# A tuned attention and SwiGLU kernel: waits at its end for the last stores alone, and 11 warming products in place of 13

## The chip, the cores and the metric

The kernel runs on one core of one Trainium2 chip. The metric is device time in microseconds; where several runs are told of, their median stands. A profile shows one further execution, its span running from its first to its last instruction. The engines are called PE (TensorE, products; PEld are its weight loads), ACT (ScalarE), DVE (VectorE), POOL (GpSimd) and SP (SyncE). SP issues nearly all DMAs; POOL issues those that add to what lies in memory.

## The reference

There are 2048 rows x of width 1024 in bfloat16. They are normalised, pass through linear attention with 32 heads of 32, and through a gated feed-forward block of inner width 3584; the result is x plus their product with a SiLU:

```python
xn  = layernorm(x)
q, k, v = heads(xn @ wqkv)                 # 32 heads of 32
pq, pk  = phi(q), phi(k)                   # phi(t) = (t+1 if t>0 else exp(t)) + 1e-6
kv  = einsum("bhsd,bhse->bhde", pk, v);  z = sum over s of pk
o   = (pq @ kv) / (pq . z + 1e-6)
s   = o.reshape(S, D) @ wo
h   = (silu(xn @ w_gate) * (xn @ w_up)) @ w_down
out = x + s * silu(h)
```

## The kernel before, in words

The kernel is not written in the order in which it runs. The builder makes a list of operations (class Op: engine, function, estimated time, what it reads and writes), and a planner (class Plan) orders it.

*The work.* All large products are done on 2 x 2 blocks with seven block products in place of four times two, and some blocks are split once more in the same way. The rows are cut into tiles of 128, normalised on DVE, POOL and ACT (ln_tile) and transposed (t_tile): the first four tiles on PE with ACT copying the result into X, the later ones by transposing DMAs. Keys and values come first, with the sums kv and z kept in PSUM; then the gate, up and query products in blocks of 512 columns; then the attention's output, written to s_scratch; last the down projection in four groups of rows. The inner values h are kept in h_scratch in DRAM, with some sums made by accumulating DMAs.

*The start.* DVE clears a small tile wz, POOL makes the identity matrix, and PE computes NWARM products of the identity with wz, 512 columns each. Their results are not used. They go around the eight PSUM banks. Behind them on PE stand the transposes of row tile 0 (L237), which read the tile that DVE normalises (L755), and then the first true products (p_piece, L230). These read the transposed tile from X, which ACT copies there (L358), and chunks of the QKV weights from H, which SP loads with the first DMAs of all (L371).

*The end.* The first three groups of the down projection add their results to the output by accumulating DMAs from POOL (dacc), out of three buffers in turn (g_ring), each with a semaphore. The output had been filled with x for them. The last group adds x on DVE and stores the sum with plain DMAs from SP, each of its stores with a semaphore of its own. Its last output tile is cut into pieces of 256, 128 and 128 columns.

*The planner.* Every operation has a due time, worked out backwards from its readers and from PE's cumulative estimated time (pecum). For loads that have a reader, the due time also decides which PE operation must have run before the load is issued. PE's operations run in the listed order within a window of ten; the other engines take, among what is ready, the one with the earliest due time, less a boost. The table BOOST gives boosts by the operation's number in the list. Each PE operation's estimate counts in two ways: with the mm_cost at which it was made in pecum, and with its field busy in the simulated clock.

*Emission.* Plan.emit turns the order into one program per engine, in which an operation stands behind the waits that its engine does not already know to be met. A wait is emitted as wait_ge by _run (L222); every operation raises a semaphore, its engine's by one or its DMA's own by 16. Plan.count has the last value of each semaphore. When all is ordered, the builder adds waits to SP's program: one for each DMA semaphore in use, in the order in which the semaphores were made, for the value in Plan.count. At the end of the block all engines meet (L254). The five programs are straight lines without loops.

Of the kernel before, what the change touches and what calls it, by code (L numbers as in the profile page):

```python
# [237 lines left out]
    return last  # L238


def build_kernel(nc, A_x, A_wqkv, A_wo, B_w_gate, B_w_up, B_w_down, out, WINDOW=10, NWARM=13, NPE=4, LEAD=16.0, CLAMP=1000.0, AHEAD=4.0):
    S, D, FF = 2048, 1024, 3584
    NT, KT, NG, NPAIR = 16, 8, 8, 14
    EPS_LN, EPS_PHI = 1e-5, 1e-6
# [9 lines left out]
    with ExitStack() as es:  # L254
# [20 lines left out]
        def named(*key):  # L275
            return Region([key])
# [6 lines left out]
        ident, ones, maskbd = (TM.at(14 * KB + 256 * q, 256, FP16) for q in range(3))  # L283
# [16 lines left out]
        ps = [es.enter_context(nc.psum_tensor("ps%d" % b, [128, 512], F32)) for b in range(8)]  # L300
        bank_r = [named("bank", b) for b in range(8)]
# [29 lines left out]
        semn = {}  # L331
# [6 lines left out]
        PL = Plan(WINDOW, LEAD, CLAMP, AHEAD)  # L338
        MM = 0.2137

        def mm_cost(mms):
            return sum(max(r.shape[-1] / 2400.0 + 0.0026, 0.03) * (o.shape[0] * r.shape[0] / 16384.0)
                       for (o, _, r, _, _) in mms)

        def pe_mm(reads, writes, mms):
            return PL.op("pe", reads, writes, partial(_mm_group, mms), mm_cost(mms))
# [60 lines left out]
        ident_r, ones_r, mask_r = (TM.reg(14 * KB + 256 * q, 256) for q in range(3))  # L407
# [72 lines left out]
        wz = TM.at(0, 1 * KB, FP16)  # L480
        wz_r = TM.reg(0, 1 * KB)
        dve([], [wz_r], lambda h: h.memset(wz, 0.0), 256)
        for n in range(NWARM):
            b = n % 8
            pe_mm([ident_r, wz_r], [bank_r[b]], [(ps[b][:, :], ident[:, :], wz, True, True)]).busy = 0.38


        XOF = {1: "R00", 2: "R10", 3: "R11", 4: "T4", 5: "T1", 6: "T2", 7: "T3"}
# [1150 lines left out]
        sp = {}  # L1639
# [81 lines left out]
        for g, c in enumerate(G):  # L1721
# [5 lines left out]
        feed(None)  # L1727
        flush()

        BOOST = {1: 5058, 29: 18306, 30: 754, 31: 18202, 32: 872, 33: 880, 34: 881, 37: 3, 39: 68, 41: -2586,  # L1730
# [7 lines left out]
        for k, v in BOOST.items():  # L1738
            PL.ops[k].boost = v
        PL.schedule()  # L1740
        prog = PL.emit(esem)
        for s in semn.values():
            if id(s) in PL.count:
                prog["sp"].append(("w", s, PL.count[id(s)]))

        @block.tensor
        def _(h):
# [19 lines left out]
def bass_recurrent_scan__linear_attn_block__swiglu_ffn__prompt_kernel(  # L1767
    nc: bass.Bass,
    A_x: bass.AP,
    A_wqkv: bass.AP,  # L1770
    A_wo: bass.AP,
    B_x: bass.AP,
    B_w_gate: bass.AP,
    B_w_up: bass.AP,
    B_w_down: bass.AP,
    out: bass.AP,
):
    build_kernel(nc, A_x, A_wqkv, A_wo, B_w_gate, B_w_up, B_w_down, out)
# [28 lines left out]
```

## Time and profile before

| | |
|---|---|
| median of 3 runs | 705.55 us (705.12 to 705.91) |
| profiled execution, its own time | 704.51 us |
| its span, first to last instruction | 702.7 us |
| PE busy | 694.8 us (99%) |
| DVE busy | 610.7 us (87%) |
| ACT busy | 424.7 us (60%) |
| POOL busy | 68.4 us (10%) |
| DMA | 103.68 MB, mean 148 GB/s |

In the profile, a line of the code such as L230 is often that of a helper: all products are recorded at L230, all transposes on PE at L237, all ACT operations at L358, SP's DMAs at L371 and POOL's at L375. Groups are told apart by the tiles that they write and read, as in out_dram<-W. The busy time counts no waits and no issues of DMAs, so an engine that executes nothing but waits is idle in it. A time of 5.24 us in a row is measured from the start of the span.

### The profile page before, as it was taken

How to read it: one execution, taken by the hardware profiler on the slowest of the kernel's cores; microseconds unless marked ns; L12 is line 12 of the kernel's file. 1: busy time of each engine (PE TensorE's matmuls, PEld its weight loads, DVE VectorE, ACT ScalarE, POOL GpSimd, SP SyncE). 2: the span in 40 equal slices, each digit the busy share in tenths (PEclk: the TensorE clock that was granted, in tenths of full speed). 3: DMA queues.
4: the chain of work that ended last, by engine and by line, in shares of the span. 5: the costliest groups of instructions: out<-in, count | busy, mean ns of one | idle time of the engine just before them, and what ended most of it. 6: DMA issues, size and time to landing. Idle time of an engine off the chain costs nothing.

```text
span 702.7 us, 11996 instructions
## 1 busy us (share of the span) xinstructions
PE 694.8 (99%) x4436; PEld 421.4 (60%) x4436; DVE 610.7 (87%) x1391; ACT 424.7 (60%) x848; POOL 68.4 (10%) x87
## 2 busy tenths in 40 slices
PE   8999999999999999999999999999999999999996
PEld 3544445555555566666666666666665448687784
DVE  6999998667999799898999999888879998768685
ACT  4877645867978967868866567775763113232222
POOL 2111000001100011020110110001101211111010
PEclk9999999999999999999999999999999999999999
DMA  9434213126612376584670486766627875666672
GB/s 313 106 83 106 54 60 121 61 90 145 155 61 69 117 195 169 174 236 101 166 194 1 106 242 198 242 218 165 165 81 225 192 182 176 155 165 156 207 180 69
DMA packets 96107, 103.68 MB, mean 148 GB/s; under 512 B 18256, under 2 KB 91344, under 8 KB 95952
## 3 DMA queue, kind: packets, MB, share of 16 engines
q1 hardware_dynamic: 84976, 92.43, 41.9%
q0 software_dynamic: 11072, 10.49, 11.9%
q8 instruction: 35, 0.57, 0.3%
q14 instruction: 24, 0.20, 0.1%
HBM read 65.54 MB, written 37.36 MB: 146 GB/s over the span
## 4 chain that ended last, share of the span: by engine, by line
PE 99%; ACT 0%; POOL 0%; DVE 0%; issue 0%; POOLq 0%
PE ps L230 99%; PE ps L237 0%; ACT X L358 0%; DVE W L368 0%; POOL TM L415 0%; ACT W L358 0%; POOL TM L414 0%; POOLq L1792 0%
## 5 line engine op out<-in xcount | busy, mean ns | idle before, releaser
L358 ACT ACTIVATE TM<-ps 128x512 f32<-128x512 f32 (+2 forms) x341 | 169.0, 528 | 50.5 <-PE ps L230 45.6
L368 DVE TENSOR_TENSOR ps<-ps,TM 128x256 f32<-128x256 f32 (+1 forms) x322 | 157.7, 509 | 40.2 <-PE ps L230 35.8
L230 PE MATMUL ps<-X,W 128*128 128x512 f16 (+1 forms) x896 | 190.4, 340 | 0.0
L230 PE MATMUL ps<-P,W 128*128 128x512 f16 (+1 forms) x896 | 188.9, 338 | 0.0
L358 ACT ACTIVATE H<-ps 128x512 f16<-128x512 f32 (+1 forms) x181 | 106.3, 601 | 55.9 <-PE ps L230 54.9
L230 PEld LDWEIGHTS ps<-X,W 128*128 128x128 f16 (+1 forms) x896 | 87.5, 98 | 59.5 <-DVE W L368 0.2
L230 PEld LDWEIGHTS ps<-P,W 128*128 128x128 f16 (+1 forms) x896 | 87.6, 98 | 58.4 <-DVE ps L368 0.2
L358 ACT ACTIVATE ps<-ps 128x256 f32<-128x256 f32 (+2 forms) x149 | 63.5, 426 | 72.5 <-PE ps L230 70.9
L230 PE MATMUL ps<-H,X 128*128 128x512 bf16 (+4 forms) x556 | 104.8, 336 | 0.5 <-ACT X L358 0.5
L368 DVE TENSOR_TENSOR H<-H 128x1024 f16<-128x1024 f16 (+5 forms) x150 | 87.1, 598 | 10.6 <-ACT H L358 8.4
L368 DVE TENSOR_TENSOR W<-W 128x256 f16<-128x256 bf16 (+6 forms) x256 | 89.1, 388 | 5.1 <-PE ps L230 2.9
L230 PE MATMUL ps<-W 128*128 128x256 f16 x512 | 90.0, 273 | 0.0
L368 DVE TENSOR_TENSOR TM<-ps,TM 128x512 f32<-128x512 f32 x99 | 67.8, 686 | 12.5 <-PE ps L230 11.5
L230 PEld LDWEIGHTS ps<-H,X 128*128 128x128 f16 x556 | 52.8, 98 | 41.6 <-ACT X L358 0.6
L375 POOL DMA_DIRECT2D h_scratch<-H x28 | 33.7, 1283 | 437.4 <-DVE H L368 197.0
L230 PEld LDWEIGHTS ps<-W 128*128 128x128 f16 (+1 forms) x512 | 50.0, 98 | 27.3 <-ACT TM L358 0.6
L230 PE MATMUL ps<-H,W 128*128 128x512 f16 (+2 forms) x280 | 63.6, 358 | 0.0
L230 PE MATMUL ps<-H 128*128 128x256 f16 (+4 forms) x432 | 60.9, 273 | 0.0
L230 PE MATMUL ps<-W,H 128*128 128x256 f16 (+1 forms) x314 | 53.5, 305 | 0.0
L358 ACT ACTIVATE H<-TM 128x512 f16<-128x512 f32 x61 | 38.3, 631 | 15.6 <-DVE TM L368 15.0
L230 PEld LDWEIGHTS ps<-H 128*128 128x128 f16 (+1 forms) x432 | 38.3, 98 | 14.6 <-ACT H L358 0.2
L368 DVE TENSOR_TENSOR H<-ps,TM 128x512 f16<-128x512 f32 (+1 forms) x59 | 40.3, 685 | 2.7 <-PE ps L230 2.5
(92 smaller groups left out, 552.1 us busy)
## 6 DMA issues: line engine op xcount, KB each, us to landing
h_scratch<-H SPq DMA_DIRECT2D x70, 256.0 KB, 3.2
X<-h_scratch SPq DMA_DIRECT2D x15, 896.0 KB, 5.2
W<-in_B_w_gate_dram SPq DMA_DIRECT2D x7, 1024.0 KB, 5.4
W<-in_B_w_up_dram SPq DMA_DIRECT2D x7, 1024.0 KB, 6.1
h_scratch<-H POOLq DMA_DIRECT2D x28, 256.0 KB, 5.7
H<-in_B_w_down_dram SPq DMA_DIRECT2D x8, 896.0 KB, 6.7
W<-in_A_x_dram SPq DMA_DIRECT2D x16, 256.0 KB, 3.1
H<-in_A_wqkv_dram SPq DMA_DIRECT2D x8, 512.0 KB, 7.9
```

Source lines behind the costliest of these rows:

```text
L230: last = h.matmul(o, l, r, start=st, stop=sp, skip_group_check=True)
L358: op = PL.op("act", reads, writes, lambda h: h.activation(o, i, func, **kw), nel(o) / 1200.0 + (0.055 if src == "ps" else 0.095))
L368: return dve(reads, writes, lambda h: h.tensor_tensor(o, a, b, op), nel(o), 1.92 if fast else 0.96)
L375: return PL.op("pool", reads, writes, lambda h: h.dma_start(o, i, accum_op=ALU.add), 1.0, sem=s, nbytes=2 * nbytes)
```

## The change

The parameter NWARM goes from 13 to 11. The estimate of each warming product is raised in the same ratio, and PE's cumulative time is set after them to what 13 gave. The keys of BOOST behind the warming products go down by two, with the same values, since there are two operations fewer ahead of them. So all other operations are planned in the same order.

At the end, SP no longer waits for every DMA semaphore. The builder goes through the planned order and keeps, for each semaphore, the last DMA that no other operation in the list depends on, moved to the end of the table each time; SP then waits for these alone, with the value that the semaphore has after that DMA. A DMA that some operation depends on was waited for by that operation, or by one that its engine knows to be behind it.

```diff
-def build_kernel(..., WINDOW=10, NWARM=13, NPE=4, LEAD=16.0, CLAMP=1000.0, AHEAD=4.0):
+def build_kernel(..., WINDOW=10, NWARM=11, NPE=4, LEAD=16.0, CLAMP=1000.0, AHEAD=4.0):
...
         for n in range(NWARM):
             b = n % 8
-            pe_mm([ident_r, wz_r], [bank_r[b]], [(ps[b][:, :], ident[:, :], wz, True, True)]).busy = 0.38
+            pe_mm([ident_r, wz_r], [bank_r[b]], [(ps[b][:, :], ident[:, :], wz, True, True)]).busy = 0.38 * 13 / NWARM
+        PL.pecum = 13 * (512 / 2400.0 + 0.0026)
...
-        BOOST = {1: 5058, 29: 18306, 30: 754, 31: 18202, ...
+        BOOST = {1: 5058, 27: 18306, 28: 754, 29: 18202, ...
...
         prog = PL.emit(esem)
-        for s in semn.values():
-            if id(s) in PL.count:
-                prog["sp"].append(("w", s, PL.count[id(s)]))
+        ends = {}
+        for o in PL.order:
+            if o.sem is not None and not o.succs:
+                ends.pop(id(o.sem), None)
+                ends[id(o.sem)] = o.ev
+        for s, _, val, _ in ends.values():
+            prog["sp"].append(("w", s, val))
```

More of the change, by code (lines that the diff above doesn't have):

```diff
@@ L238, in _tr_group, with build_kernel @@
     return last
-def build_kernel(nc, A_x, A_wqkv, A_wo, B_w_gate, B_w_up, B_w_down, out, WINDOW=10, NWARM=13, NPE=4, LEAD=16.0, CLAMP=1000.0, AHEAD=4.0):
+def build_kernel(nc, A_x, A_wqkv, A_wo, B_w_gate, B_w_up, B_w_down, out, WINDOW=10, NWARM=11, NPE=4, LEAD=16.0, CLAMP=1000.0, AHEAD=4.0):
     S, D, FF = 2048, 1024, 3584
@@ L1728, in build_kernel @@
         flush()
-        BOOST = {1: 5058, 29: 18306, 30: 754, 31: 18202, 32: 872, 33: 880, 34: 881, 37: 3, 39: 68, 41: -2586,
[7 rows of a table removed]
+        BOOST = {1: 5058, 27: 18306, 28: 754, 29: 18202, 30: 872, 31: 880, 32: 881, 35: 3, 37: 68, 39: -2586, 40: 6519, 44: 4544, 47: 3050, 49: 459, 58: 181, 76: 407, 78: 3, 102: 60, 115: 570, 121: 103, 140: 3, 150: 3, 159: -3, 164: 60, 165: 150, 205: 60, 226: 8, 284: -20, 301: 60, 710: 8, 970: 8, 1059: 60, 1112: 174, 1310: 1408, 1941: 60, 1943: 3, 1949: 60, 1963: 146, 2027: 357, 2051: 150, 2315: 8, 2324: 20, 2328: 8, 2441: 76, 2456: 3, 2483: 3, 2558: 74, 2574: 3, 3352: 860, 3354: 867, 3409: 542, 3421: 238, 3471: 2362, 3495: 360, 3505: 8, 3551: -13, 3613: -34, 3641: -16, 3642: 40, 3645: 22, 3646: 87, 3647: 598, 3651: 511, 3654: 3, 3661: 2334, 3676: 1031, 3757: 213, 3779: 850, 3787: 142, 3788: 341, 3800: 113, 3823: 5058, 3825: -15, 3827: 8, 3838: 230, 3843: 2664, 3844: 2018, 3847: 8364}
         for k, v in BOOST.items():
```

7 rows, old and new, of the table BOOST are left out of this document.

## The prediction

> **What bounds the kernel now.** I read the page's head and the chain that ended last first, because they say which engine a change has to shorten. Of the chain in order of time, these are the pieces that matter here (start, length, what):
>
> ```profile
> span 702.7 us, 11996 instructions
> PE 99%; ACT 0%; POOL 0%; DVE 0%; issue 0%; POOLq 0%
> ```
>
> ```profile
> 1.43 5.59 PE ps L230 x13
> 7.01 0.24 PE ps L237 x4
> 7.28 0.60 ACT X L358
> 7.93 2.80 PE ps L230 x12
> 10.73 0.45 PE ps L237 x8
> 11.17 8.77 PE ps L230 x40
> ...
> 125.02 571.73 PE ps L230 x3755
> ...
> 697.08 0.24 DVE W L368
> ...
> 697.34 0.23 DVE W L368
> ```
>
> TensorE is the chain from 7.93 us to 696.75 us. Nothing in this change touches that stretch except through its two ends, so the question is only when TensorE's stream gets going and what happens after its last product. The chain view stops at the last computing instruction, 697.34 + 0.23 = 697.57 us, yet the span is 702.7 us: 5.1 us are missing from it. They are no engine's work, as the busy times by stretch show (columns: length, then PE, PEld, DVE, ACT, POOL with counts, granted clock, DMA share, GB/s):
>
> ```profile
> 698.30:699.40 1.10, 0.00 (x0) 0.00 (x0) 0.00 (x0) 0.00 (x0) 0.00 (x0) 1.00 0.27 60
> 699.40:702.70 3.30, 0.00 (x0) 0.00 (x0) 0.00 (x0) 0.00 (x0) 0.00 (x0) 0.54 0.01 2
> ```
>
> In the last 3.3 us no engine computes and the DMA engines are 1% busy. What runs there is found by asking for two lines of the code: L222, the wait of the emitted programs, in the last 6 us, and L254, the end of the block, where all engines meet.
>
> ```profile
> L222 SPq EVENT_SEMAPHORE  x59: 17/28/28, 698.4 to 702.2; - x59
> ```
>
> ```profile
> L254 SPq COMPARE_BRANCH  x1: 41/41/41, 702.3 to 702.3; - x1
> L254 SPq DRAIN  x1: 7/7/7, 702.5 to 702.5; - x1
> L254 SPq EVENT_SEMAPHORE  x1: 17/17/17, 702.6 to 702.6; - x1
> ```
>
> ```profile
> L254 PEldq EVENT_SEMAPHORE  x1: 51/51/51, 702.6 to 702.6; - x1
> ```
>
> So SyncE executes 59 wait instructions one after the other from 698.4 to 702.2 us, then branches, drains and meets the other engines, which have long been at the meeting point. (702.2 − 698.4) / 58 = 66 ns for each, although each lasts 17 to 28 ns. The end of the span is a queue of waits, and the stores they wait for are older:
>
> ```profile
> 697.40 0.43 SPq L371 DMA_DIRECT2D out_dram<-W  x1
> ```
>
> ```profile
> 697.87 0.43 SPq L371 DMA_DIRECT2D out_dram<-W  x1
> ```
>
> ```profile
> out_dram<-W SPq DMA_DIRECT2D x1, 32.0 KB, 1.5
> ```
>
> The last store is issued at 697.87 us and lands 1.5 us after its issue, at 699.4 us (the third row is the answer for that one issue; KB, us to landing). From 699.4 us on, SyncE is only walking through semaphores that already stand at their value.
>
> **The end, part by part.** The change replaces one wait per DMA semaphore by one wait for each semaphore whose last store has no reader in the program. By the code these are the output stores: three semaphores of the accumulating stores (the ring g_ring has three places) and one for each store of the last group. The page's table of issues counts the latter:
>
> ```profile
> out_dram<-W POOLq DMA_DIRECT2D x24, 128.0 KB, 3.8
> out_dram<-W SPq DMA_DIRECT2D x7, 128.0 KB, 1.7
> out_dram<-W SPq DMA_DIRECT2D x1, 64.0 KB, 2.0
> out_dram<-W SPq DMA_DIRECT2D x2, 32.0 KB, 1.5
> ```
>
> 7 + 1 + 2 = 10 stores by SyncE, so at most 13 wait instructions stay, put in the order of their last issue. Loads, scratch stores and the copies of x to the output all have a consumer that waited for them. At 66 ns the 13 take 0.86 us: SyncE would have walked through all but the last by 698.4 + 0.8 = 699.2 us and then stands at the last store's semaphore until 699.4 us. What is late next is thus that landing. Behind the wait nothing is queued on SyncE but the branch and the meeting, and all four other engines wait for that. From the last wait at 702.2 us to the end at 702.7 us it took 0.5 us; the same tail after 699.4 us ends the span at 699.9 us. Gain: 702.7 − 699.9 = **2.8 us**. The lower bound is given by the cover that goes: before, every landing up to 702.2 us was free. Had the last store taken as long as the slowest of the last five (3.0 us, the row below), it would land at 700.9 us and the gain would be 1.3 us. The upper bound would be a landing that costs nothing; then the walk itself, ending at 699.2 us, would set the end, for 3.0 us.
>
> ```profile
> 695.19 0.33 SPq L371 DMA_DIRECT2D out_dram<-W  x1
> ```
>
> ```profile
> out_dram<-W SPq DMA_DIRECT2D x1, 128.0 KB, 3.0
> ```
>
> I take 1.5 us for the landing, because it is what both 32 KB stores took and the 3.0 us belong to a store of 128 KB.
>
> **The start.** Two of the 13 warming products go. These rows are TensorE's weight loads and products there, and VectorE's normalised tile that the first transposes read:
>
> ```profile
> 5.67 0.15 PEld L230 LDWEIGHTS ps<-TM 128*128 128x128 f16 x1 [0.28 <-issue]
> 6.10 0.15 PEld L230 LDWEIGHTS ps<-TM 128*128 128x128 f16 x1 [0.28 <-issue]
> 6.52 0.15 PEld L237 LDWEIGHTS ps<-TM,W 128*128 128x128 f16 x1 [0.28 <-DVE W L755]
> 6.85 0.43 PEld L237 LDWEIGHTS ps<-TM,W 128*128 128x128 f16 x7 [0.18 <-issue]
> ...
> 9.67 0.56 PEld L230 LDWEIGHTS ps<-H,X 128*128 128x128 f16 x4 [0.34 <-issue]
> ```
>
> ```profile
> 5.78 0.73 DVE L755 TENSOR_SCALAR W<-W,mv,rstd 128x512 f16<-128x512 bf16 x2 [0.69 <-POOL rstd L749]
> ```
>
> A product starts about every 0.43 us, the 11th at 5.67 us, the 13th at 6.52 us, the transposes at 6.85 us. With 11 the transposes may start when the first half of the tile is there, some 0.4 us after 5.78 us. So they come about 0.6 us sooner, the second half of them behind the tile's second half (5.78 + 0.73 = 6.51 us), and the first true product (7.93 us) 0.4 to 0.6 us sooner. This gain is then lost to the weights. The chunks of the QKV weights were issued by SyncE at 2.75 and 3.30 us and landed 6.8 and 7.8 us later:
>
> ```profile
> 2.75 0.51 SPq L371 DMA_DIRECT2D H<-in_A_wqkv_dram  x1
> ```
>
> ```profile
> H<-in_A_wqkv_dram SPq DMA_DIRECT2D x1, 512.0 KB, 6.8
> ```
>
> ```profile
> 3.30 0.68 SPq L371 DMA_DIRECT2D H<-in_A_wqkv_dram  x1
> ```
>
> ```profile
> H<-in_A_wqkv_dram SPq DMA_DIRECT2D x1, 512.0 KB, 7.8
> ```
>
> One lands at 9.55 us, and the weight load that reads it starts at 9.67 us. The next lands at 11.1 us, and the following run of products starts at 11.1 us as well (11.17 in the chain). No wait on TensorE stands before these issues, so they don't move. TensorE simply waits longer at 9.6 and at 11.1 us. Gain at the start: 0, with bounds of 0.1 us gain (11.17 − 11.1) and the loss below. The renumbered boosts and the larger planned cost per product (11 × 0.449 = 13 × 0.38) keep the planner's sums, so the order costs nothing; two products and their weight loads less on TensorE's queue are counted in the above.
>
> **The clock.** The warming products exist for it. 13 products of 512 columns take 5.59 us, 430 ns each, while the 12 of 512 columns from 7.93 us take 2.80 us, 233 ns each with a wait among them. So TensorE runs at half speed first, and the step from 6.52 to 6.85 us, 0.33 us instead of 0.43 (slow) or 0.22 (fast), puts the change at about 6.74 us: 0.22 us at the slow rate are half a product, the other half takes 0.11. At the end the granted clock over 699.40 to 702.70 us is 0.54; with 1.0 before and 0.5 after, the fall to a half is at 699.40 + 0.04 / 0.5 × 3.3 = 699.66 us. By the first change TensorE had been busy without a hole for 6.74 − 1.43 = 5.3 us. With 11 products the same 5.3 us hold a hole of at most 0.2 us, between the 11th product's end at 6.1 us and the first transposes at some 6.25 us. Whether a hole of that size counts no row shows; 0.2 of 5.3 us is 4%, so I take no loss, and the second rival has its price.
>
> [...]
>
> **The sum.** The profiled execution took 704.51 us, 1.81 us more than its span, and these 1.81 us lie outside what is changed. 704.51 − 2.8 − 0 = 701.7 us in the profiled state, with a span of 699.9 us. The three runs have a median of 705.55 us (705.12 to 705.91), so the profiled one was 1.04 us below it. Taken from the median the forecast is 705.55 − 2.8 = 702.75 us, put as **702.7 us**. A measurement of this kernel can tell about 0.2%, 1.41 us, from no change: faster means below 704.14 us.
>
> **The rivals.**
> *A landing or another short stall takes the place of the walk.* In unprofiled runs the last store may land as late as the 3.0 us row. For it speaks that the rows above run from 1.5 to 3.0 us; against it that the stores issued after the slow one, of 64 and 32 KB, took 2.0 and 1.5 us. Gain 1.3 us, 704.2 us, just inside no change; landings between give 702.8 to 704.2.
> *The clock comes late.* Suppose the hole makes the busy stretch begin anew, 5.3 us from the transposes at 6.25 us: the clock comes at 11.6 us. Then from about 7.4 us on 9.8 of the 12 products run at 0.43 us, the other 2.2 at 0.22, and the eight transposes take 0.45: 12.5 us instead of 11.1, a loss of 1.4 us, and 704.1 us in all, at the edge of no change. If the wait at 9.6 us breaks it again, the clock comes near 16.9 us: twelve products at 0.43 and eight transposes at 0.11 end at 13.4 us, a loss of 2.3 us, and half of the 3.5 us from there is lost too, 4.0 us together: 706.7 us. That is the case on the other side, slower. It outweighs the end once the clock is later than some 14.4 us, and is slower by 0.2% past 17.2 us. For it: nothing but the shorter warming. Against it: the hole's 4%, and that from 11.17 us on the chain shows TensorE without a pause.
> *The waits cost nothing in unprofiled runs.* If the 66 ns were a matter of the profiler, the walk would be over by the landing at 699.4 us and nothing would change: 705.5 us. Against it: the profiled execution was no longer than the others.
>
> **How the numbers follow.** Forecast as summed, 702.7 us with its own range 702.0 to 703.4: 0.72. A later landing or short stall, half of its span still faster by 0.2%: 0.13 (0.10 faster, 0.03 same). Clock late: 0.09, of which by less than the 1.4 us 0.06, faster; by more 0.03, same. Clock late a second time: 0.02, slower. Walk free: 0.04, of which 0.03 same and 0.01 slower by chance of the draw. Faster 0.88, same 0.09, slower 0.03. The range goes from 701.6 us (the profiled execution less 2.8 us, with the start's 0.1) to 704.2 us (the slow landing).
>
> **What would show it.** L222 on SyncE has at most 13 waits after the last store's issue, the last ending within 0.1 us of the landing; the span ends 0.5 us behind it, at 699.9 us. The first true product starts at 7.4 to 7.6 us, and the run after the second set of transposes still at 11.1 us; from there every TensorE start is where it was. Wrong if products after 8 us are still 0.43 us apart, if the last landing is past 700.4 us, or if the tail behind the last wait is longer than 0.5 us.

## The result, and the profile after

The changed kernel takes 702.29 us in the median of six runs (702.08 to 702.47), the kernel before 705.25 us beside it (six runs, 704.91 to 705.91). The ratio is 0.9957, with a 95% interval of 0.9945 to 0.9969; ratios here and below are worked out from all runs, and so differ a little from those of the medians. The forecast was 702.7 us. The profiled execution took 702.29 us, with a span of 700.6 us.

SyncE's waits at the end (L222), in the view of that line over the last microseconds, are now these; below them is the end of the block (L254):

```profile
L222 SPq EVENT_SEMAPHORE  x5: 17/27/28, 699.0 to 700.1; - x5
```

```profile
L254 SPq COMPARE_BRANCH  x1: 41/41/41, 700.2 to 700.2; - x1
L254 SPq DRAIN  x1: 13/13/13, 700.3 to 700.3; - x1
...
L254 PEldq EVENT_SEMAPHORE  x1: 51/51/51, 700.5 to 700.5; - x1
```

Five wait instructions are left of 59. Their 1.1 us from the first to the last are no walk any more; SyncE stands there until the stores land. Two of the last three stores follow, the one of 64 KB with its row of the view of DMA issues (us from issue to landing at its end), and the very last:

```profile
697.03 1.01 SPq L371 DMA_DIRECT2D out_dram<-W  x1
```

```profile
out_dram<-W SPq DMA_DIRECT2D x1, 64.0 KB, 2.4
```

```profile
698.55 0.43 SPq L371 DMA_DIRECT2D out_dram<-W  x1
```

The last one is issued at 698.55 us and lands 1.5 us later, at 700.1 us, and the span ends 0.5 us behind that: the landing has taken the place of the walk. But it lies 0.7 us later than the 699.4 us of before. Two things made it so. The store of 64 KB needed 1.01 us for its issue, where it had been 0.60 us. And TensorE ran some 0.26 us later throughout, as the chain that ended last shows from its beginning (start, length, what):

```profile
2.75 7.08 DMA H<-in_A_wqkv_dram
9.83 0.14 issue
9.96 1.02 PE ps L230 x4
10.99 0.45 PE ps L237 x8
11.43 2.29 PE ps L230 x10
...
690.18 6.84 PE ps L230 x62
...
697.61 0.22 DVE W L368
```

The chain now begins with a load of weights, not with the warming. TensorE's own rows at the start, from the timeline:

```profile
1.43 4.36 PE L230 MATMUL ps<-TM 128*128 128x512 f16 x11 [1.43 <-POOL TM L415]
6.61 0.72 PE L237 MATMUL ps<-TM,W 128*128 128x128 f16 x8 [0.81 <-DVE W L756]
7.69 1.90 PE L230 MATMUL ps<-H,X 128*128 128x512 bf16 x8 [0.37 <-ACT X L358]
9.96 1.02 PE L230 MATMUL ps<-H,X 128*128 128x512 bf16 x4 [0.37 <-DMA H<-in_A_wqkv_dram]
10.82 0.61 PE L237 MATMUL ps<-TM,W 128*128 128x128 f16 x8
11.39 6.88 PE L230 MATMUL ps<-H,X 128*128 128x512 bf16 x30
```

The first true product starts at 7.69 us instead of 7.93, the run behind the second transposes at 11.39 us instead of 11.13. The fourth weight chunk, issued at 3.30 us, took 8.0 us to land instead of 7.8:

```profile
H<-in_A_wqkv_dram SPq DMA_DIRECT2D x1, 512.0 KB, 8.0
```

So two questions were open: whether the smaller warming made the loads later, and what lengthens the issue of a store.

### The profile page after: what moved, and what is told of

It is laid out like the page before. It is cut to its first block, busy times and chain, and to the rows that moved or that the text cites. A ratio compares the mean times of both kernels' runs of the same rounds, so it can differ in the third digit from the quotient of the medians.

```text
span 700.6 us, 11917 instructions
## 1 busy us (share of the span) xinstructions
PE 692.9 (99%) x4413; PEld 421.0 (60%) x4434; DVE 610.9 (87%) x1391; ACT 424.7 (61%) x848; POOL 68.5 (10%) x87
## 4 chain that ended last, share of the span: by engine, by line
PE 98%; DMA 1%; SPq 0%; issue 0%; ACT 0%; DVE 0%
PE ps L230 98%; DMA H<-in_A_wqkv_dram 1%; PE ps L237 0%; SPq L371 0%; ACT H L358 0%; ACT ps L358 0%; DVE W L368 0%; ACT W L358 0%
## 5 line engine op out<-in xcount | busy, mean ns | idle before, releaser
L230 PE MATMUL ps<-H,X 128*128 128x512 bf16 (+4 forms) x545 | 103.1, 335 | 1.3 <-DMA H<-in_A_wqkv_dram 0.4
L368 DVE TENSOR_TENSOR TM<-ps,TM 128x512 f32<-128x512 f32 x99 | 68.0, 687 | 12.4 <-PE ps L230 11.5
```

Source lines behind the costliest of these rows:

```text
L230: last = h.matmul(o, l, r, start=st, stop=sp, skip_group_check=True)
L368: return dve(reads, writes, lambda h: h.tensor_tensor(o, a, b, op), nel(o), 1.92 if fast else 0.96)
```

## The experiments

The theory: the walk of waits is the whole gain; the start is worth nothing, because TensorE's stream starts when the fourth weight chunk lands. The rival: the 11 products carry part of the gain, or cost something by later loads.

**Each part alone.** Only the end:

```diff
-NWARM=11      # and its two lines of estimates, and BOOST's keys
+NWARM=13
```

> 13 warming products, waits for the last stores alone. Theory (the walk of waits is the whole gain, the start gives nothing): 702.3 us, as the full change, ratio 0.9957; SyncE has 5 to 7 waits after the last store's issue, and the run of products after the second set of transposes starts when its weight chunk lands, at 11.1 to 11.4 us. Rival (the start with 11 products carries part of it): between 702.6 and 705.3 us.

Measured: 702.44 us, ratio 0.9964 (0.9951 to 0.9976). SyncE has five waits, as expected:

```profile
L222 SPq EVENT_SEMAPHORE  x5: 17/28/28, 699.4 to 700.5; - x5
```

The run behind the second transposes starts at 11.89 us, later than the 11.1 to 11.4 us expected, because the chunk landed later. Only the warming, with the old waits:

```diff
-        ends = {} ...
-        for s, _, val, _ in ends.values():
-            prog["sp"].append(("w", s, val))
+        for s in semn.values():
+            if id(s) in PL.count:
+                prog["sp"].append(("w", s, PL.count[id(s)]))
```

> 11 warming products, one wait per semaphore at the end as before. Theory: 705.3 us, ratio 1.000 within 0.001; the first true product starts near 7.7 us in place of 7.93, and nothing of that is left at the run of products that begins at 11.1 to 11.4 us. Rival (start carries part): 704.6 to 705.0 us. Rival (fewer products make the first loads land later, as 9.83 and 11.34 us in the changed kernel against 9.57 and 11.09 us): 705.5 us or more, with the landing at 11.3 us again.

Measured: 705.16 us, ratio 1.0002 (0.9994 to 1.0011). The kernel before had 704.71 us in 21 runs beside it, and 705.15 us in eleven further ones (below), so medians of the same kernel differ by 0.4 us. SyncE's walk was there again, and with it the time from the last product to the end of the span:

```profile
L222 SPq EVENT_SEMAPHORE  x59: 17/28/28, 698.1 to 701.9; - x59
```

```profile
696.71:702.40 5.69, 0.00 (x0) 0.00 (x0) 0.58 (x3) 0.28 (x1) 0.00 (x0) 0.83 0.16 48
```

The end is the gain, the warming has none that can be measured. In the second kernel the fourth chunk landed 7.8 us after its issue, as in the kernel before, and with 13 products in the first it took 8.5 us. In these two profiles fewer products thus don't make the loads later; the table below has all of them.

**The waits on an idle engine.** The waits that the change drops, at the end of GpSimd's program:

```diff
+        for s in semn.values():
+            if id(s) in PL.count and id(s) not in ends:
+                prog["pool"].append(("w", s, PL.count[id(s)]))
```

> As the changed kernel, with the 105 or so waits that it drops put at the end of GpSimd's program instead. GpSimd issues its last store near 674 us and then does nothing. Theory (what cost was that SyncE walked through them after the last store's landing): 702.3 us as the changed kernel, the walk lies in GpSimd's idle time apart from waits for the loads of the last tiles. Rival (it is the number of waits or semaphores as such, wherever they stand): 705.3 us.

Measured: 702.54 us, ratio 0.9966 (0.9954 to 0.9979). GpSimd had the waits behind it 7 us before the last product:

```profile
L222 POOLq EVENT_SEMAPHORE  x54: 17/43/43, 674.9 to 690.6; - x54
```

On an idle engine the waits cost nothing that can be measured. What cost was that they stood on SyncE behind its last store.

**The kernel before, once more.**

> The kernel before, unchanged, for a second profile: 705.3 us. Theory (the first profile, 704.51 us, was a lucky one): a span nearer 703.4 than 702.7 us, with the third weight chunk landing later than 11.09 us or a longer issue of the last stores; SyncE's walk again 3.8 us from its first wait to its last. Rival (the profiled span is always 702.7 us and the rest lies outside it): 702.7 us again.

Measured: 705.15 us, ratio 1.0005 (0.9996 to 1.0014), with a span of 703.1 us, half way between the 702.7 us of the first profile and the 703.4 us expected. The walk was again 3.9 us long. The fourth chunk landed 8.4 us after its issue at 3.31 us. The first profile of before had indeed met an early landing. In the kernel with GpSimd's waits it came later than anywhere: 9.2 us after 3.30 us, at 12.5 us, and TensorE's run behind the second transposes starts there (chunk's landing, then the rows of TensorE's first run behind it and of its last):

```profile
H<-in_A_wqkv_dram SPq DMA_DIRECT2D x1, 512.0 KB, 9.2
```

```profile
12.56 5.80 PE L230 MATMUL ps<-H,X 128*128 128x512 bf16 x25
...
695.79 2.38 PE L230 MATMUL ps<-H,X 128*128 128x256 bf16 x34
```

From that start to the last product's end it is 698.17 − 12.56 = 685.6 us; in the changed kernel 697.02 − 11.39 = 685.6 us; in the kernel before 696.75 − 11.13 = 685.6 us. A difference in the landing of one chunk thus passes through to the end of the last product without loss.

**The long issue.** What remains is the time from the last product to the end of the span. In the profiles with a long issue of a store, the view of DMA queues shows one packet of 0.02 MB on the instruction queue q8 at that time; here the changed kernel, 696.2 to 697.6 us, and the kernel with the old waits and 11 products, 695.7 to 698.0 us, in which all issues took 0.33 to 0.44 us:

```profile
q1 hardware_dynamic: 270, 0.25, 51.4%
q8 instruction: 1, 0.02, 6.1%
...
out_dram<-W SPq DMA_DIRECT2D x1, 128.0 KB, 2.9
```

```profile
q1 hardware_dynamic: 432, 0.33, 43.4%
...
out_dram<-W SPq DMA_DIRECT2D x1, 128.0 KB, 1.7
```

The last store of 128 KB lands after 2.9 us in the first and after 1.7 us in the second.

In the trace of before q8 has 35 such packets in the span, 213 to 284 of TensorE's instructions apart, 256 in the mean. Theory: such a fetch belongs to TensorE's program, and an issue of a store that falls into it can last until the fetch is over. Two kernels move the fetch by the number of TensorE's instructions alone. The first cuts two of the 11 products into halves, so that the program is as long as with 13; the second cuts each into four:

```diff
 # e5_split_two, for the products n = 0 and 1
-[(ps[b][:, :], ident[:, :], wz, True, True)]
+[(ps[b][:, c:c + 256], ident[:, :], wz[:, c:c + 256], True, True) for c in (0, 256)]
 # e6_fetch_early, for all
-[(ps[b][:, :], ident[:, :], wz, True, True)]
+[(ps[b][:, 128 * q:128 * q + 128], ident[:, :], wz[:, 128 * q:128 * q + 128], True, True) for q in range(4)]
```

> The changed kernel; two of its 11 warming products are cut into halves of 256 columns, so that TensorE's program has as many instructions as with 13, while the warming takes as long as with 11. Theory (near the end a 16 KB fetch of TensorE's instructions falls where its program crosses a page, and SyncE's issue of a store that overlaps it lasts until some 0.3 us after the fetch): fetch 0.9 to 1.0 us before TensorE's last product ends, as in the three profiles with 13, one store's issue of 0.5 to 1.1 us in place of 0.33 to 0.43, and 3.2 to 3.6 us from the last product to the end of the span. Rival (a matter of warming or of chance): issues of 0.33 to 0.43 us and 2.9 us as in the last profile with 11.

> The changed kernel; each of its 11 warming products is cut into four of 128 columns, 66 instructions more on TensorE in the same time. Theory (the fetch stalls the issue): the fetch comes some 3.5 us earlier, at 692 to 693 us, and meets a store that isn't last; the last four stores are issued in 0.33 to 0.43 us each, and the span ends 2.9 us after the last product in place of 3.56, about 0.5 us faster than the changed kernel in the mean, 701.8 to 702.2 us. Rival (the long issue has another cause): 0.6 to 1.1 us for one of the last issues again, 702.3 to 702.5 us.

Measured: 702.16 us, ratio 0.9961 (0.9948 to 0.9975), and 701.79 us, ratio 0.9956 (0.9944 to 0.9969). In the first, the fetch and a long issue are there (queue view of 695.5 to 697.1 us, SyncE's row):

```profile
q8 instruction: 1, 0.02, 5.7%
```

```profile
696.51 0.90 SPq L371 DMA_DIRECT2D out_dram<-W  x1
```

In the second, the fetch comes between 690 and 693 us, none lies between 695 and 699 us, and the same store's issue is short:

```profile
697.00 0.33 SPq L371 DMA_DIRECT2D out_dram<-W  x1
```

The stretches from the last product's end to the end of the span, one row of the view by stretch for each kernel: the changed one, the one cut into halves, the one cut into four:

```profile
697.01:700.57 3.56, 0.00 (x0) 0.00 (x0) 0.57 (x3) 0.28 (x1) 0.00 (x0) 1.00 0.27 76
```

```profile
696.49:699.96 3.47, 0.00 (x0) 0.00 (x0) 0.58 (x3) 0.28 (x1) 0.00 (x0) 0.83 0.28 78
```

```profile
696.98:699.86 2.88, 0.00 (x0) 0.00 (x0) 0.58 (x3) 0.28 (x1) 0.00 (x0) 1.00 0.32 91
```

In these two kernels the fetch moves with TensorE's program, and the long issue goes with the fetch. The same stands elsewhere in the traces. In the kernel before, a fetch runs from 492.03 to 493.19 us, and the store that SyncE begins to issue meanwhile takes 1.52 us, until 0.4 us after it (queue view of 492 to 493 us, SyncE's row):

```profile
q8 instruction: 1, 0.02, 7.2%
```

```profile
492.06 1.52 SPq L371 DMA_DIRECT2D h_scratch<-H  x1
```

Between 30 and 690 us of all 14 profiles, 222 of SyncE's DMA_DIRECT2D issues overlap a fetch on q8, and 52 of them take over 0.9 us; of the 3257 others 19 do. Of the 67 over 0.6 us that overlap one, 61 end 0.3 to 0.53 us after the fetch. So most issues within a fetch are not long, but those that are end with it.

**Fewer warming products still.** With 5 and with 1:

```diff
-NWARM=11
+NWARM=5       # e8_warm_1: 1; BOOST's keys accordingly
```

> The changed kernel with 5 warming products in place of 11. Theory (the stream is set by the landing of the fourth weight chunk): the warming ends at 3.6 us, the clock is at full speed by 10 us or so, and the time is 702.3 us as with 11, plus at most 0.7 us for a late clock. Rival (the clock's switch needs the busy stretch and comes late): products 0.43 us apart until 11 us or later, 703.5 us or more.

> The changed kernel with one warming product. Theory: as with 5; the clock cannot switch before TensorE has worked through the first true products, so that these 12 are 0.43 us apart and end near 13 us: 703 to 705 us. Rival (the start is set by the weights whatever the clock is): 702.3 us.

Measured: 702.99 us, ratio 0.9974 (0.9964 to 0.9985), and 702.85 us, ratio 0.9971 (0.9959 to 0.9983). With 5, TensorE's timeline:

```profile
7.88 4.40 PE L230 MATMUL ps<-H,X 128*128 128x512 bf16 x12 [0.26 <-ACT X L358]
12.11 0.61 PE L237 MATMUL ps<-TM,W 128*128 128x128 f16 x8
12.56 5.77 PE L230 MATMUL ps<-H,X 128*128 128x512 bf16 x26
```

The 12 products take 4.40 us instead of 2.80, so the clock came late: up to the transposes at 12.11 us it is 4.23 us, which are 7.8 products at 0.427 us and 4.2 at 0.216 us, and that puts it at 7.88 + 3.3 = 11.2 us. The fourth chunk had landed at 3.30 + 8.1 = 11.4 us, and the run behind the transposes starts at 12.56 us: 1.1 us lost. The 10 us expected for the full clock and the 0.7 us at most for a late one were my estimates; this run shows 11.2 and 1.1 us in their place. No fetch fell on the stores, which gave back 0.7 us (2.90 us from the last product to the end). A late clock, the second rival of the prediction, thus did come with 5 products. In the profile with 1 the clock was late too (12 products in 4.26 us, which end at 11.9 us and not near 13), but the chunk landed at 3.29 + 9.0 = 12.3 us, and the run started at 12.32 us: nothing was lost there. With 5, 702.99 us is at the limit of what was expected; with 1, 702.85 us is under the 703 to 705 us expected.

**The fetch out of the way, with 13 products; and the changed kernel again.** The first is the end-only kernel with each of its 13 products cut into four.

> 13 warming products, each cut into four of 128 columns, and waits for the last stores alone: the run with early fetch, but with the warming of before. Theory (with the fetch out of the way, the number of warming products is worth nothing, since the stream starts at the landing of the fourth weight chunk): 701.8 us, within 0.3 us of the run with 11 and early fetch; last four stores issued in 0.33 to 0.43 us, 2.9 us from the last product to the end. Rival (13 are slower by the 0.4 to 0.6 us that the first products come later): 702.2 to 702.4 us.

Measured: 702.14 us (701.55 to 702.88), ratio 0.9961 (0.9949 to 0.9974). This lies 0.35 us above the 701.79 us with 11, just outside the 0.3 us expected and just under the 702.2 us of the rival. Medians of one kernel differ as much, so it separates nothing, the less as the profile with 13 had another loss: from the run behind the transposes to the last product's end it is 686.2 us instead of 685.6. The chain has a load of rows there that landed 9.37 us after its issue at 9.08 us, and the transposes wait for the tile that is normalised from these rows:

```profile
22.72 0.62 PE L237 MATMUL ps<-TM,W 128*128 128x128 f16 x8 [0.41 <-ACT W L358]
```

> The changed kernel, unchanged, for a second profile. If the fetch near the end is fixed by the program: 0.7 us before the last product's end, a store's issue of 0.6 us or more and 3.4 to 3.6 us from the last product to the end, as in its first profile. If it differs between executions (as the profiles with 11 and the old end or GpSimd's walk suggest, where it came 1 us after the span): 2.9 us from the last product to the end, and a time 0.5 us shorter for the same landing of the fourth weight chunk.

Measured: 702.21 us, ratio 0.9961 (0.9947 to 0.9974). The fetch was there, with a long issue and 3.28 us to the end:

```profile
696.66 0.71 SPq L371 DMA_DIRECT2D out_dram<-W  x1
```

Last, the changed kernel and the one cut into four beside each other on one chip.

> The changed kernel beside the run with early fetch, on one chip. If the fetch near the end is fixed by the program: again some 0.72 us before the last product's end, and 3.3 to 3.6 us from there to the end of the span; 702.2 us.

> The run with early fetch, again, beside the changed kernel on the same chip. Theory: 2.9 us from the last product's end to the end of the span, and a median 0.4 to 0.7 us under the changed kernel's, 701.7 us. Rival (its first time was a lucky draw of the landing of the weights): the same median as the changed kernel within 0.2 us.

Measured: 702.02 us (701.77 to 702.50) and 702.16 us (701.68 to 702.68); ratios 0.9960 (0.9946 to 0.9973) and 0.9959 (0.9946 to 0.9971). This time the changed kernel had no fetch near its end, and both have the same stretch behind the last product (the changed one, then the one cut into four):

```profile
697.05:699.95 2.90, 0.00 (x1) 0.00 (x0) 0.58 (x3) 0.28 (x1) 0.00 (x0) 1.00 0.31 90
```

```profile
698.08:700.97 2.89, 0.00 (x0) 0.00 (x0) 0.58 (x3) 0.28 (x1) 0.00 (x0) 1.00 0.32 91
```

So my expectation that the fetch is fixed by the program fell: the same program had it before its end in two profiles and not in the third. And the kernel cut into four isn't measurably faster than the changed one; its first 701.79 us may have owed much to the landing (11.3 us in its first profile, 12.4 us in its second). All 14 profiles in one table, in us; "landing" is that of the fourth chunk, "rest" the time from the last product's end to the end of the span, "fetch" whether a fetch lay within 1 us ahead of the last product's end:

| kernel | products | old waits | landing | fetch | rest |
|---|---|---|---|---|---|
| before | 13 | yes | 11.1 | yes | 5.96 |
| before again | 13 | yes | 11.7 | yes | 5.73 |
| warming only | 11 | yes | 11.1 | no | 5.69 |
| changed | 11 | no | 11.3 | yes | 3.56 |
| changed, second | 11 | no | 11.0 | yes | 3.28 |
| changed, third | 11 | no | 11.4 | no | 2.90 |
| end only | 13 | no | 11.8 | yes | 3.39 |
| waits on GpSimd | 11 | no | 12.5 | no | 2.90 |
| two halved | 11 | no | 10.8 | yes | 3.47 |
| cut into four | 11 | no | 11.3 and 12.4 | no | 2.88 and 2.89 |
| 13, cut into four | 13 | no | 11.3 | no | 2.90 |
| with 5 | 5 | no | 11.4 | no | 2.90 |
| with 1 | 1 | no | 12.3 | no | 2.90 |

The landing has the same mean, 11.5 us, over the four profiles with 13 products and the eight with 11.

## Why the prediction was right

*The end.* The walk, its place and its price were as forecast. Without a fetch the rest is 5.69 us with the walk and 2.90 us without: 2.8 us, the predicted sum. With a fetch the pairs give 5.96 or 5.73 against 3.28 to 3.56, 2.2 to 2.7 us, because the fetch did not lengthen the same issue by the same amount each time. Take from each rest what the issue of the 64 KB store took above 0.33 us (0.27 and 0.04 us of the kernel before, 0.68 and 0.38 us of the changed one), and it is 5.69 us with the walk and 2.88 to 2.90 us without. The measured medians differ by 2.96 us in the first comparison, and by 2.2 to 2.9 us in those of the end alone, of the waits on GpSimd and of the changed kernel again. Fewer waits were left than the bound of 13: ten, one for each of SyncE's stores. The accumulating stores have none, since a later use of their buffer waits for them. In the trace a wait instruction holds up to two semaphores, so the ten are five instructions and the branch, and the 59 instructions and the branch of before held 118; it is 108 that went, and not some 105 as the expectation of the run with GpSimd's waits has it. The 66 ns are a mean: in each of the three walks there is one pause of 0.36 to 0.38 us from one wait to the next, and the others have a mean of some 61 ns. The 0.5 us behind the last wait held.

*The rival of the landing.* It happened in part, but by the issue ahead of the last store, not by the landing, which stayed at 1.5 us in every profile. The row of 0.60 us for that issue stood in the trace of before and was not used. The walk did not cover it: it starts when the last store has been issued, and 5.96 − 5.69 = 0.27 us is what this issue took above 0.33. This is the step that was mis-sized: "a landing or another short stall" cost 0.4 to 0.7 us in the profiles with a fetch. The 3.0 us of the slow landing were put down to the 128 KB of that store; without a fetch, stores of 128 KB land in 1.7 us (the row of the kernel with the old waits and 11 products).

*The start.* The gain of 0 held, for the reason given: the first products came sooner (7.69 us against 7.93) and waited at the weights (9.96 and 11.39 us). They came a little later than the 7.4 to 7.6 us forecast, because the transposes waited for the normalised tile until 6.61 us and not 6.25. That TensorE's starts would be "where they were" from 11.1 us on was wrong by what the landing differs between executions: 10.8 to 12.5 us over these profiles.

*The sum.* The 1.04 us between the profiled execution of before and the median were taken as they stood. The second profile of before, 0.35 us longer in its span with the landing 0.6 us later and the rest 0.2 us shorter, shows where such differences come from. That 702.7 us came so near to 702.29 has some luck in it: the median of three runs from which it starts, 705.55 us, lies 0.3 to 0.8 us above all other medians of the kernel before (704.71 to 705.25).

*The clock.* It was not late in any profile with 11 products, as forecast, but the reason given for it did not hold. The prediction took a hole of at most 0.2 us in a busy stretch of 5.3 us. The hole was 0.81 us in the changed kernel and 1.28 us in the one with the warming alone:

```profile
1.43 3.86 PE L230 MATMUL ps<-TM 128*128 128x512 f16 x11 [1.43 <-POOL TM L415]
6.58 0.72 PE L237 MATMUL ps<-TM,W 128*128 128x128 f16 x8 [1.28 <-DVE W L756]
```

Nor does the clock need 5.3 us. At 0.43 us each the 11 products would take 4.7 us; they took 3.86 us, since the trace's record of the clock has it full from 4.13 us on, 2.7 us after the first product. Over the profiles this record has the change at 4.1 to 5.9 us with 11 products, at 6.5 to 6.7 us with 13, at 11.2 us with 5 and 10.6 us with 1. In the 13 profiles that have both of its ends, the stretch at full clock lasted 689.49, 692.91 or 696.32 us (with 5 products, in the first profile of before and in the changed kernel, for example), in steps of 3.41 us. In each of the 13, the 3.41 us before the change to full clock hold at least 2.70 us of busy TensorE (the least in the kernel with the warming alone, 0.72 to 4.13 us), and each stretch of 3.41 us counted back from there holds at most 2.31 us (the most with 5 products, 0.98 to 4.39 us). In the two kernels above, the hole came behind the change: the clock was full at 5.15 and 4.13 us, and the 11 products ended at 5.79 and 5.29 us. So it was not a small hole that kept the clock in time. What decides the time of the change is not shown beyond these numbers, nor whether the clock is late in some execution with 11. The chance of 0.06 for a clock late by less than 1.4 us was my estimate; no profile with 11 products shows such a delay. With 5 products the clock was late, and that cost 1.1 us in the profile.

## What to carry to other kernels

Look at what lies between the last computing instruction and the end of the span: it is not in the chain, and wait instructions that are already met still cost some 66 ns each here when one engine executes them in a row behind its last store. Wait there only for what nobody has waited for, or put the other waits on an engine that has long been idle. And before costing a saving ahead of a stream of products, look whether the stream's start is set by a landing: then the saving is slack, as long as the clock comes in time (4.1 to 5.9 us here with 11 products, 11.2 us with 5), and the landing's own spread (10.8 to 12.5 us here) goes into every measurement.

## What was not expected of the hardware

A fetch of instructions lengthened the issue of stores by another engine. In the profiles with a fetch near the end, one SyncE issue took 0.60 to 1.10 us instead of 0.33 to 0.43 us in five of six; in the sixth (before again) the fetch was over as the last three issues began, and they took 0.37 to 0.44 us. Issues within a fetch are long elsewhere in the traces too, in about a quarter of the cases (52 of 222 over 0.9 us). TensorE had no pause while one packet of 0.02 MB came on q8 (busy for all of the 0.73 us from the packet's start at 696.27 us to the last product's end at 697.00 us in the changed kernel); the engine that issues stores meanwhile was held up, by 0.68 us for the store of 64 KB there. How the one holds up the other is not shown, and why the same program of 11 products has its last fetch sometimes before and sometimes behind its end stays open.
